# RG-LRU scan and soft mixture of experts: the input gate of the first four token blocks by tanh, their product on VectorE, and a new instruction order

## The chip, the cores and the metric

One core of a Trainium2 chip runs the whole program. The metric is device microseconds from launch to end. Engines are named as the profile names them: PE is TensorE, DVE is VectorE, ACT is ScalarE, POOL is GpSimd, and SP is the queue that issues the DMAs.

## The reference, cut to what matters

```python
# x, r_gate, i_gate: (4, 5056, 256) float32; a_param: (256,)
a_base = 1 / (1 + exp(-a_param))
sig_r, sig_i = sigmoid(r_gate), sigmoid(i_gate)
a_t  = exp(8 * sig_r * log(a_base))
norm = sqrt(maximum(1 - a_t * a_t, 1e-6))
x_gated = norm * sig_i * x
for t in range(S):                      # a linear recurrence along each sequence
    h = a_t[:, t] * h + x_gated[:, t];  y[:, t] = h
# soft mixture of experts over the N = 20224 tokens of y: 8 experts, 4 slots each
logits = y @ phi                        # (N, 32)
slots = softmax_over_tokens(logits).T @ y
slot_out[e] = relu(slots[e] @ w1[e]) @ w2[e]
out = softmax_over_slots(logits) @ slot_out
```

## The kernel before

The 20224 tokens are cut into 40 blocks of 512 (the last has 256). A block lies in memory with tokens on the partitions, and the scan wants channels there, so PE transposes. What is done for block w, with its name in the plan and the line that does it in the profile:

- `Lr`, `Li`, `Lx`: SP loads r, i and x, 512 KB each (L382).
- `rp`, `sr`: PE transposes r, four transposes for each half of the channels (L397); ACT takes the gate from PSUM (L409).
- `si`: ACT takes the input gate in place, untransposed (L420).
- `ex`: ACT makes a = exp(8 sig_r log a_base) (L462, or L460 where the gate was a sigmoid).
- `sq`, `qr`: POOL squares a (L471), 128x1024 in SBUF; ACT takes the root of 1 - a*a (L478).
- `u`: POOL multiplies gate and x (L432), 128x1024, both operands in SBUF.
- `up`, `st`, `sc`: PE transposes that product (L490); DVE multiplies it in PSUM with the root, held at 1e-3 or more (L500), and scans (L513); each for the two halves.
- `yp`, `yc`: PE transposes y back (L533), and DVE or ACT copies it out of PSUM (L288 on DVE, L286 on ACT).

Logits and the running softmax over tokens follow for each four blocks. After the last block come the sum of the slots, the experts (PE, weights loaded during the first part), and for every token the softmax over slots, the product with the slots' outputs (L894), the copies (L288, L286), and the write of 20.7 MB (L912).

ACT works on **units** of one or two blocks: `si`, `ex` and `qr` are each done once for a unit. The functions lie in three tables, sigmoid, exponential and root; tanh is to be had with the sigmoid and with the exponential. The gate of r is written for both: as a sigmoid while the sigmoid's table is in force, else as tanh(r/2) with the half put into `ex`. `TANH_I` lists the units whose input gate is done likewise; it is empty here. The branch for it is in the code (`twice`): the gate is tanh(i/2), which may run in the exponential's phase; the product is (1 + tanh) * x, one DVE instruction that reads two tiles in SBUF; this is twice the product wanted, so the root is taken of 0.25 - 0.25 a*a, and its floor is halved.

Nothing at run time sets the order. `ORDER` is a list of 1243 numbers: the operations in the order in which they are emitted, a `b` choosing the second engine where two are possible. Each engine, and SP, works off its own in that order. The buffers are given out by `Plan.take` along the same list: SBUF has 38 for tiles of 512 KB (a unit of two blocks takes a pair), PSUM has eight banks. An operation that takes a buffer waits until the last operation on its former content is done; on SP, all later loads wait behind it.

Of the kernel before, what the change touches and what calls it, by code (L numbers as in the profile page):

```python
# [26 lines left out]


ORDER = """
# [15 lines left out]
507 431 592 508 529 299b 852 530 531 532 611 613 612 614 472 858 509 510 318 354 376 373 355 377 391 411 432 452  # L45
473 392 493 320 337 359 339 319 321 859 374 361 340 360 362 338 465 487 424 464 627 486 446 648 730 415 378 380
393 412 381 396 860 861 733 653 397 413 398 862 394 416 430 711 587 609 505 527 506 528 451 379b 433 474 470 395
417 414 492 471 713 630 631 654 712 714 511 864 865 437 456 871 872 438 457 439 453 434 632 478 873 458 435 454
436 479 455 866 735 867 875 868 475 595 633 736 513 734 876 863 869 418 399 401 459 461 419b 402b 460b 554 476
480 477 651 420 497 870 400 462 498 421 512 533 516 481 519 483 482 499 494 596 514 534 616 652 874 555 575 515  # L50
597 556 495 484 496 877 878 879 538 880 520 440 441 517 442 535 882 536 518 521 443 539 540 537 881 522 667 500
883 670 502 668 588 610 628 546 689 568 975 672 649 789 811 547 569 552 553 690 629 650 989 749 770 523b 634 671
593 541 574 503 884 501 557 560 816 561 543 562 558 544 886 792 542b 673 674 692 576 693 559 594 885 793 887 598
579 601 635 615 655 752 888 889 890 753 580 602 581 577 603 599 578 775 694 794 620 891 621 600 622 717 776 817
814 795 695 773 774 815 617 563 565 566 676 618 892 619 604 582 893 584 583 894 524 638 636 656 637 718 738 677
697 585 895 606 657 641 605b 525b 607b 564b 719 678 660 754 623 897 625 639 658 642 640 710 709 731 669 732 691
790 812 963 986 965 750 771 969 985 751 772 643 661 659 662 675 715 696 682 679 904 905 626 680 683 906 716 756
898 755 737 757 701 908 698 681 684 699 702 700 703 723 720 899 900 739 901 902 624b 798 685 686b 663 664b 909
704 644 705b 665 687 646 896 645b 666b 688b 647b 758 778 759 721 724 722 725 740 799 819 800 742 743 741 903 910
760 911 706 912 707 744 915 913 763 916 726 745 777 779 782 761 764 762 796 747 917 919 765 780 783 781 784 746b  # L60
727b 748b 766 768 728 1089 767b 920 918 729b 978 977 966 791 971 813 979 962 987 983 968 959 957 797 801 804 921
818 820 922 923 924 823 805 802 907 769b 914 803 806 974 972 961 824 821 825 822 982 981 958 988 960 967 976 973
964 980 984 970 785 1067 926 927 786b 807 928 787 937 938 808b 929 788 930 939 946 931 826 827b 940 947 809 810b
941 932 933 942 948 949 943 934 944 935 1090 950 1068 925 951 945 936 952 1013 1111 1035 953 1177 954 1091 990
1112 1113 1000 1114 991b 1036 1014 1037 1038 1039 995 992 996 1005 1001 997 1002 993 1069 1015 1070 1115 1016
1006 1092 998 1071 1017 994 1003 999 1007 1008 1004 1009 1178 1093 1179 1010 955 1116 1040 1018 1094 1072 1041
956 1011 1073 1042 1074 1180 1012b 1055 1056 1057 1059b 1058b 1043 1049 1044 1047 1050 1053 1046b 1045b 1061
1095 1052b 1065b 1096b 1062b 1063b 1051 1181 1064 1075 1076b 1077b 1079 1078 1082 1199 1019 1083b 1086b 1084b
1085 1200 1020 1201 1182 1104 1155 1105b 1107 1156 1097 1157 1133 1108b 1202 1106b 1098b 1099b 1028 1029b 1032b
1031b 1117 1101 1100 1134 1135 1030 1118b 1021 1022b 1024b 1136 1158 1119 1221 1183 1120b 1184b 1122b 1123b 1025  # L70
1023 1121 1159 1160 1126 1161 1127b 1162b 1129b 1128b 1222 1223 1130 1137 1185 1186 1203 1170 1189b 1187b 1188b
1138 1192 1171 1174b 1173b 1224 1172b 1193 1204 1196 1139 1163 1140b 1194b 1195b 1148 1164 1167 1165 1225 1149
1150 1205 1226 1151b 1152b 1166 1206b 1214 1215 1218 1217 1216b 1060 1048 1054 1066 1227 1228b 1141 1207 1208b
1209b 1210b 1142 1143 1145 1211 1144 1229 1236 1230 1231 1237 1240 1233 1239 1238b 1232b 1080 1081 1087 1088
1110 1103 1109 1033 1102 1034 1026 1124 1027 1125 1131 1132 1175 1191 1190 1176 1153 1197 1168 1220 1219 1147
1213 1198 1242 1234 1235 1146 1154 1212 1169 1241
"""


# [11 lines left out]
class Plan:  # L91
# [84 lines left out]
def kernel(  # L176
# [56 lines left out]
    def Bk(key):  # L233
        return banks[plan.place[key]]
# [4 lines left out]
    def halves(key):  # L239
        return G(key).rearrange("p (h t) -> p h t", h=H)  # L240
# [116 lines left out]
    def window(w):  # L357
# [136 lines left out]
                    )  # L494
            return emit

        def e_st(h):
            def emit(o):
                up = Bk(("up", w, h))[:, :c]
                nc.vector.scalar_tensor_tensor(  # L500
                    up, halves(("N", w))[:, h, :c], 5e-4 if twice else 1e-3, up, op0=ALU.max, op1=ALU.mult
                )
            return emit

        cuts = [0] + [b * S - w * C for b in range(1, B) if w * C < b * S < w * C + c] + [c]

        def e_sc(h):
            def emit(o):
                up = Bk(("up", w, h))
                for s0, s1 in zip(cuts[:-1], cuts[1:]):  # L510
                    init = 0.0 if (w * C + s0) % S == 0 else last_col[h]
                    dst = halves(("A", w))[:, h, s0:s1]
                    nc.vector.tensor_tensor_scan(  # L513
                        dst, dst, up[:, s0:s1], init, op0=ALU.mult, op1=ALU.add
                    )
                    last_col[h] = halves(("A", w))[:, h, s1 - 1 : s1]
            return emit

        for h in range(H):
            op(("up", w, h), "PE", 0.5 * f, e_up(h), deps=[("u", w), ("ident",)],  # L520
               alloc=[("B", ("up", w, h))], uses=[("x", w)])
            op(("st", w, h), "DVE", 0.06 + 0.54 * f, e_st(h), deps=[("up", w, h), ("qr", u0)],
               uses=[("N", w), ("up", w, h)])
            op(("sc", w, h), "DVE", 0.09 * (len(cuts) - 1) + 1.09 * f, e_sc(h),
               deps=[("st", w, h), ("sc", w - 1, h)],
               uses=[("A", w), ("up", w, h)] + ([("A", w - 1)] if w else []))

        def e_yp(i):
            def emit(o):
# [436 lines left out]
```

## Time and profile before

| | |
|---|---|
| median of 3 runs | 301.55 us (301.49 to 302.47) |
| the profiled execution | 301.67 us, span of its instructions 299.8 us |
| busy in the span | PE 234.7, DVE 239.7, ACT 242.2, POOL 181.9 us |
| bytes moved | 100.03 MB, mean 334 GB/s |
| ACT table loads | 24 |

The profile is of one execution. Busy time is a share of the whole span, but the span has three parts: blocks come in and are scanned, up to about 216 us; the experts, to about 245 us; and the output, to the end. Lines that are not quoted in the prediction are left out here.

### The profile page before, as it was taken

The numbers are of one execution on the slowest core, as the hardware profiler recorded it, in microseconds if no ns is written. First come the engines' busy times: TensorE is split into PE (matmuls) and PEld (weight loads), VectorE is DVE, ScalarE is ACT, GpSimd is POOL, SyncE is SP. The second block draws the span as 40 slices with busy tenths as digits, with TensorE's granted clock in tenths as the row PEclk, the third lists the DMA queues.
The fourth block names the chain that finished last, engine by engine and source line by source line (L and its number), as shares of the span: only waits on it lengthen the run. The fifth ranks groups of instructions, "written<-read, shape, count | busy, mean of one in ns | idle before, by whom it ended". The sixth has DMA issues, their size and how long they took to land.

```text
span 299.8 us, 5788 instructions
## 1 busy us (share of the span) xinstructions
PE 234.7 (78%) x2140; PEld 166.0 (55%) x2140; DVE 239.7 (80%) x379; ACT 242.2 (81%) x303; POOL 181.9 (61%) x122
## 2 busy tenths in 40 slices
PE   3605788869896989799958996899999999898200
PEld 3505575666773967457647663557573677665100
DVE  1003999899999999989999999999968779889600
ACT  5899999999999999999999999999323248885100
POOL 4299579988498898899749898798000421121000
PEclk9975999979999899979999999999999999999755
DMA  6999999799895988859998789999991019999997
GB/s 247 416 410 407 410 397 382 306 390 359 327 416 206 416 340 330 302 200 382 331 360 318 273 302 404 385 378 380 339 398 60 3 79 402 404 402 407 404 378 297
DMA packets 28032, 100.03 MB, mean 334 GB/s; under 512 B 3362, under 2 KB 3364, under 8 KB 28004
## 3 DMA queue, kind: packets, MB, share of 16 engines
q1 hardware_dynamic: 28004, 99.66, 86.7%
q8 instruction: 17, 0.28, 0.4%
q14 instruction: 11, 0.09, 0.1%
HBM read 78.94 MB, written 20.71 MB: 332 GB/s over the span
## 4 chain that ended last, share of the span: by engine, by line
ACT 28%; PE 27%; POOL 15%; issue 12%; DVE 7%; DMA 4%; DVEq 0%; POOLq 0%; ACTq 0%
POOL g L471 8%; POOL g L432 5%; ACT g L462 4%; ACT g L420 4%; ACT g L478 4%; PE b L397 4%; ACT y L286 4%; ACT g L409 4%; PE b L894 4%; DMA g<-in_x_dram 4%; PE b L533 3%; PE b L490 3%; DVE g L288 3%; PE b L788 2%; PE b L761 2%
## 5 line engine op out<-in xcount | busy, mean ns | idle before, releaser
L432 POOL TENSOR_TENSOR g<-g 128x1024 f32<-128x1024 f32 (+1 forms) x40 | 92.7, 2344 | 18.9 <-ACT g L420 17.2
L513 DVE TENSOR_TENSOR_SCAN g<-g,b 128x512 f32<-128x512 f32 (+4 forms) x86 | 98.7, 1175 | 0.4
L471 POOL TENSOR_TENSOR g<-g 128x1024 f32<-128x1024 f32 (+1 forms) x40 | 73.8, 1873 | 17.9 <-ACT g L462 13.6
L500 DVE SCALAR_TENSOR_TENSOR b<-g,b 128x512 f32<-128x512 f32 (+1 forms) x80 | 51.8, 675 | 25.1 <-PE b L490 24.1
L490 PE MATMUL b<-ident,g 128*128 128x128 f32 x316 | 48.5, 289 | 22.0 <-POOL g L432 20.2
L490 PEld LDWEIGHTS b<-ident,g 128*128 128x128 f32 x316 | 36.3, 146 | 35.0 <-POOL g L432 23.6
L397 PE MATMUL b<-ident,g 128*128 128x128 f32 x316 | 46.7, 293 | 6.0 <-DMA g<-in_r_gate_dram 3.7
L533 PE MATMUL b<-ident,g 128*128 128x128 f32 x316 | 44.7, 284 | 8.3 <-DVE g L513 6.8
L397 PEld LDWEIGHTS b<-ident,g 128*128 128x128 f32 x316 | 37.9, 151 | 15.7 <-issue 4.2
L533 PEld LDWEIGHTS b<-ident,g 128*128 128x128 f32 x316 | 35.8, 144 | 18.8 <-DVE g L513 11.2
L409 ACT ACTIVATE g<-b 128x512 f32<-128x512 f32 (+1 forms) x80 | 42.4, 604 | 2.9 <-PE b L397 2.9
L861 POOL TENSOR_TENSOR y<-y,rs 128x512 f32<-128x512 f32 x10 | 10.4, 1047 | 53.5 <-DVE g L779 25.2
L462 ACT ACTIVATE g<-g,ca 128x1024 f32<-128x1024 f32 (+2 forms) x30 | 39.1, 1371 | 0.0
L420 ACT ACTIVATE g<-g 128x2048 f32<-128x2048 f32 (+2 forms) x22 | 37.9, 1744 | 0.1
L478 ACT ACTIVATE g<-g 128x2048 f32<-128x2048 f32 (+2 forms) x22 | 36.8, 1732 | 0.1
L288 DVE COPY y<-b 128x512 f32<-128x512 f32 x53 | 34.6, 680 | 2.1 <-PE b L533 1.5
L286 ACT COPY g<-b 128x512 f32<-128x512 f32 (+1 forms) x45 | 22.2, 567 | 8.7 <-PE b L894 8.0
L894 PE MATMUL b<-soR,y 32*128 32x256 f32 x320 | 27.2, 405 | 1.2 <-ACT y L286 0.7
L288 DVE COPY g<-b 128x512 f32<-128x512 f32 (+1 forms) x43 | 24.7, 629 | 2.5 <-ACT y L286 0.8
L286 ACT COPY y<-b 128x512 f32<-128x512 f32 x36 | 20.0, 601 | 5.7 <-PE b L533 4.4
L621 PE MATMUL b<-y,e 128*32 128x257 f32 x316 | 22.9, 388 | 1.2 <-ACT e L612 1.2
L579 PE MATMUL b<-g,phi_sb 128*32 128x512 f32 (+1 forms) x160 | 22.4, 622 | 0.0
(86 smaller groups left out, 220.2 us busy)
## 6 DMA issues: line engine op xcount, KB each, us to landing
g<-in_i_gate_dram SPq DMA_DIRECT2D x39, 512.0 KB, 7.1
g<-in_x_dram SPq DMA_DIRECT2D x39, 512.0 KB, 6.5
out_dram<-g SPq DMA_DIRECT2D x39, 512.0 KB, 6.4
g<-in_r_gate_dram SPq DMA_DIRECT2D x38, 512.0 KB, 6.5
g<-in_moe_w_dram SPq DMA_DIRECT2D x32, 512.0 KB, 6.2
g<-in_r_gate_dram SPq DMA_DIRECT2D x3, 256.0 KB, 5.0
g<-in_i_gate_dram SPq DMA_DIRECT2D x1, 256.0 KB, 4.2
g<-in_x_dram SPq DMA_DIRECT2D x1, 256.0 KB, 7.7
```

Source lines behind the costliest of these rows:

```text
L286: nc.scalar.copy(out=dst, in_=srct)
L288: nc.vector.tensor_copy(out=dst, in_=srct)
L397: nc.tensor.transpose(out=by_tile(rp, n)[:, j, :], in_=rows(("r", w), n)[:, j, h * P : (h + 1) * P], identity=ident,)
L409: nc.scalar.activation(halves(("A", w))[:, h, :c], Bk(("rp", w, h))[:, :c], f, scale=k)
L420: nc.scalar.activation(a, a, AF.Tanh if twice else AF.Sigmoid, scale=0.5 if twice else 1.0)
L432: nc.gpsimd.tensor_tensor(out=rows(("x", w), n), in0=rows(("i", w), n), in1=rows(("x", w), n), op=ALU.mult)
L462: nc.scalar.activation(a, a, AF.Exp, scale=ca[:, h : h + 1], bias=ca[:, h : h + 1])
L471: nc.gpsimd.tensor_tensor(out=halves(("N", w))[:, :, :c], in0=a, in1=a, op=ALU.mult)
L490: nc.tensor.transpose(out=by_tile(up, n)[:, j, :], in_=rows(("x", w), n)[:, j, h * P : (h + 1) * P], identity=ident,)
L500: nc.vector.scalar_tensor_tensor(up, halves(("N", w))[:, h, :c], 5e-4 if twice else 1e-3, up, op0=ALU.max, op1=ALU.mult)
L513: nc.vector.tensor_tensor_scan(dst, dst, up[:, s0:s1], init, op0=ALU.mult, op1=ALU.add)
L533: nc.tensor.transpose(out=yp[:, j, h * P : (h + 1) * P], in_=halves(("A", w))[:, h, (2 * i + j) * P : (2 * i + j + 1) * P], identity=ident,)
```

## The change

The units are now {0}, {1}, {2, 3}, {4, 5} and so on in twos; before they were {0}, {1, 2}, {3, 4}, {5}, {6, 7} and so on. The first three, blocks 0 to 3, have their input gate by tanh: `si` runs in the exponential's phase, `u` is one DVE instruction for each block, and `qr` carries the quarter. A path that would put the floor and the product with the root on POOL (`BY_POOL`) is written in and used for no block. `ORDER` is new throughout. The lines move: L429 is the product on DVE, L433 POOL's, L410 the gate of r, L421 `si`, L463 `ex`, L472 the square, L479 the root, L491 `up`, L504 `st`, L528 `sc`, L289 the copy on DVE.

```diff
-UNITS = [1] + [2] + [2, 1] + [2] * 17
-TANH_I = []
+UNITS = [1, 1] + [2] * 19
+TANH_I = [0, 1, 2]
 EXM = [(12, 14), (18, 20), (30, 34), (36, 38)]
+BY_POOL = []
 ORDER = """
-5 1 33 55 11 115 74 96 116 34 13 56 12 75 97 138 35 137 57 178 200 76 159 98 219 241 160 179 201 117 0 3 6 7 8 9
...
+5 1 0 3 6 7 8 9 10 11 14 16 15 12 18 17 33 36 38 37 39 20 55 58 96 60 99 101 77 82 80 118 121 59 100 102 83 42
...
+        pooled = w in BY_POOL
+        least = 5e-4 if twice else 1e-3
+
         def e_st(h):
...
-                    up, halves(("N", w))[:, h, :c], 5e-4 if twice else 1e-3, up, op0=ALU.max, op1=ALU.mult
+                    up, halves(("N", w))[:, h, :c], least, up, op0=ALU.max, op1=ALU.mult
...
+            if pooled:
+                continue
```

The new order at the places that the prediction speaks of (`g` is a tile in SBUF, `b` a bank of PSUM, `ca` the constants of the channels). ACT from its last `ex` ahead of the first root, before (the r gate's tanh of block 4 is L409 here, `ex` of blocks 3 and 4 the second L462):

```order
L409 ACTIVATE g<-b_73 128x512
L462 ACTIVATE g<-g,ca 128x512 x2
L462 ACTIVATE g<-g,ca 128x2x512 x2
L420 ACT_TABLE_LOAD
L420 ACTIVATE g<-g 128x1024
L420 ACTIVATE g<-g 128x2048
L478 ACT_TABLE_LOAD
L478 ACTIVATE g<-g 128x1024
L478 ACTIVATE g<-g 128x2048
L420 ACT_TABLE_LOAD
```

and the same place now (L463 is `ex`, L421 `si`, L479 `qr`; the first L463 here is blocks 2 and 3, the last blocks 4 and 5):

```order
L410 ACTIVATE g<-b_74 128x512
L463 ACTIVATE g<-g,ca 128x2x512 x2
L421 ACTIVATE g<-g 128x1024
L421 ACTIVATE g<-g 128x2048
L463 ACTIVATE g<-g,ca 128x2x512 x2
L479 ACT_TABLE_LOAD
L479 ACTIVATE g<-g,quarter 128x1024 x2
L479 ACTIVATE g<-g,quarter 128x2048
L479 ACTIVATE g<-g 128x2048
L421 ACT_TABLE_LOAD
```

The load of the sigmoid's table ahead of the first root is gone; the gates of block 1 and of blocks 2 and 3 stand among the exponentials (block 0's is the second ACT instruction after the constants), and the roots of blocks 0 to 5 follow each other as before.

DVE from its first instruction on a block, before (the 128x512 with a bank `b` are `st`, L500, and `sc`, L513, which is listed under the name of its kind):

```order
L334 TENSOR_SCALAR ca<-ca 128x2
L500 SCALAR_TENSOR_TENSOR b_72<-g,b_72 128x512
L500 SCALAR_TENSOR_TENSOR b_73<-g,b_73 128x512
L513 SCALAR_TENSOR_TENSOR g<-g,b_73 128x512
L513 SCALAR_TENSOR_TENSOR g<-g,b_72 128x512
L500 SCALAR_TENSOR_TENSOR b_76<-g,b_76 128x512
```

and now:

```order
L335 TENSOR_SCALAR ca<-ca 128x2
L429 SCALAR_TENSOR_TENSOR g<-g 128x1024 x4
L504 SCALAR_TENSOR_TENSOR b_74<-g,b_74 128x512
L504 SCALAR_TENSOR_TENSOR b_76<-g,b_76 128x512
L528 SCALAR_TENSOR_TENSOR g<-g,b_74 128x512
L504 SCALAR_TENSOR_TENSOR b_73<-g,b_73 128x512
```

The four products, of blocks 0, 2, 3 and 1 in this order, stand ahead of every `st`, so a late product is a late scan.

POOL from its first square, before (L471 the squares of blocks 1, 2, 0, 5 and 3, L432 the products):

```order
L471 TENSOR_TENSOR g<-g 128x1024 x5
L432 TENSOR_TENSOR g<-g 128x1024 x2
L471 TENSOR_TENSOR g<-g 128x1024
L432 TENSOR_TENSOR g<-g 128x1024 x6
L471 TENSOR_TENSOR g<-g 128x1024 x6
```

and now (L472 the squares of blocks 0 to 3, then 4 and 5; six small memsets stand between):

```order
L472 TENSOR_TENSOR g<-g 128x1024 x4
L297 MEMSET y_62 128x4
...
L472 TENSOR_TENSOR g<-g 128x1024 x2
L433 TENSOR_TENSOR g<-g 128x1024 x4
L472 TENSOR_TENSOR g<-g 128x1024 x6
```

POOL has four products fewer, and its last squares of this stretch, blocks 2 to 5, fall into the time of DVE's products.

On SP the loads begin r0, i0, r1, r2, r4, r3, r5, r6, i1, x2, i2, i3, x0, r8, x3, x1, r7, r14, i4 (the number is the block); before they began r1, r2, r0, r5, r3, r4, i5, i1, x0, i2, i0, i3, i4, i6, x1. By the buffers that `Plan.take` gives out, i4 and i5 go to the pair that held i2 and i3, which `u` of blocks 2 and 3 read last; before, none of the first 29 loads waited for a product. In the first part DVE makes 48 of the 79 copies `yc` and ACT 31; before it was 50 and 29. The table loads are 23.

More of the change, by code (lines that the diff above doesn't have):

```diff
@@ L50 @@
[L50 to L64, printed above, removed]
@@ new lines @@
+453 454 458 692 865 875 671 633 693 713 714 513 672 554 673 863 874 876 734 494 475 455 495 476 477 496 533 512
+866 867 868 497 478 479 480 869 399 516 401 418 420 514 534 595 421b 515 555 575 556 596 616 597 498 870 402 440
+442 459 400 419 460 461 499 443 877 878 879 880 462 881 441 519 520 517 518 481 694 483 484 538 882 539 521 883
+535 500 501 502 536 668 547 588 690 610 546 587 628 609 568 649 789 811 629 569 540 537 884 792 749 669 650 770
+552 553 560 557 503b 593 793 695 482b 634 814 541 574 576 579 886 752 542b 674 561 558 559 577 562 578 594 598
@@ new lines @@
+664b 646 647b 626b 685 687 688b 909 907 666b 706 707b 739 742 721 725 686 722 740 743 741 744 758 778 759 799
+819 777 800 796 760 910 763 911 912 913 914 915 916 761 764 762 917 745 726 728 779 747 782 919 765 780 783 781
+784 727b 729b 746b 1089 766 768 920 918 748b 769b 767b 988 989 967 791 979 959 970 977 960 975 962 984 966 981
+813 963 987 797 801 804 818 957 802 805 803 921 922 923 924 820 785 787 806 821 823 824 825 822 926 1067 927 928
+807 937 938 1090 939 946 925 1068 971 976 958 964 968 985 961 974 978 980 965 982 788b 786b 808b 826 930 931 827
@@ new lines @@
+941 947 809 810b 948 932 933 949 934 929 942 935 1091 950 940 951 936 943 944 945 952 1177 1111 1013 953 1035
+1069 1178 954 990 995 991 1179 1036 1112 1014 1015 1180 996 1000 992 997 993 1005 1113 1114 1001b 994 1037 998
+1038 1006 1181 1007 1002 1003 1008 999 1004 1009 1070 1016 1092 1093 1071 1039 1115 1010 955 956 1072 1040 1094
+1041 1011 1012b 1073 1074b 1042 1043 1044b 1047 1045 1046b 1055 1061 1056b 1058b 1059 1057 1063 1065 1049 1053
+1062b 1052b 1064b 1050b 1095 1017 1051 1096b 1075 1076b 1077b 1079 1078 1116 1018 1082 1133 1083b 1086b 1085b
@@ new lines @@
+1084 1134 1199 1135 1200 1104 1105 1107 1019 1117 1136 1137 1106b 1020b 1108b 1118b 1201 1097 1098b 1101b 1221
+1138 1182 1139 1140b 1099 1100 1222 1223 1028 1202 1029b 1031b 1030 1032 1126 1141 1127 1128 1130b 1129b 1203
+1119 1142b 1145b 1224 1143b 1144 1155 1120 1156 1157 1204 1205 1122b 1225 1226 1206b 1121b 1123b 1021 1148 1022b
+1149b 1024 1152b 1227 1183 1228b 1025 1151 1150 1023 1184b 1158 1214 1215 1217 1218b 1216b 1207 1048 1060 1066
+1054 1208 1209 1210b 1211b 1185 1236 1186b 1188 1187 1237 1189b 1240b 1229 1159 1238 1230 1231 1239 1232b 1233b
@@ L77 @@
+1160 1161 1192 1162b 1193b 1195b 1170 1194b 1196 1163 1171b 1173b 1172b 1174 1164 1165b 1166b 1167b 1081 1080
+1087 1088 1110 1109 1103 1102 1034 1132 1131 1033 1147 1124 1146 1125 1154 1026 1219 1212 1220 1190 1153 1235
+1213 1198 1234 1242 1241 1176 1168 1027 1197 1169 1175 1191
 """
@@ L500, in emit, with e_uc, e_nm, e_pb @@
                 nc.vector.scalar_tensor_tensor(
-                    up, halves(("N", w))[:, h, :c], 5e-4 if twice else 1e-3, up, op0=ALU.max, op1=ALU.mult
+                    up, halves(("N", w))[:, h, :c], least, up, op0=ALU.max, op1=ALU.mult
                 )
             return emit
+        def e_uc(h):
+            return lambda o: copy(o, halves(("x", w))[:, h, :c], Bk(("up", w, h))[:, :c])
+        def e_nm(o):
+            nt = halves(("N", w))[:, :, :c]
+            nc.gpsimd.tensor_scalar(nt, nt, least, None, op0=ALU.max)
+        def e_pb(o):
+            b = halves(("x", w))[:, :, :c]
+            nc.gpsimd.tensor_tensor(out=b, in0=halves(("N", w))[:, :, :c], in1=b, op=ALU.mult)
         cuts = [0] + [b * S - w * C for b in range(1, B) if w * C < b * S < w * C + c] + [c]
@@ L526, in window @@
                uses=[("A", w), ("up", w, h)] + ([("A", w - 1)] if w else []))
+        if pooled:
+            op(("nm", w), "POOL", 0.08 + 0.95 * f, e_nm, deps=[("qr", u0)], uses=[("N", w)])
+            for h in range(H):
+                op(("uc", w, h), ("ACT", "DVE"), {"DVE": 0.06 + 0.54 * f, "ACT": 0.055 + 0.43 * f}, e_uc(h),
+                   deps=[("up", w, 0), ("up", w, 1)], uses=[("x", w), ("up", w, h)])
+            op(("pb", w), "POOL", 0.08 + 1.77 * f, e_pb, deps=[("nm", w), ("uc", w, 0), ("uc", w, 1)],
+               uses=[("N", w), ("x", w)])
+            for h in range(H):
+                op(("sc", w, h), "DVE", 0.09 * (len(cuts) - 1) + 1.09 * f, e_sc(h),
+                   deps=[("pb", w), ("sc", w - 1, h)], uses=[("A", w), ("x", w)] + ([("A", w - 1)] if w else []))
         def e_yp(i):
```

29 lines of the change are left out of this document (10 added, 19 removed), and 29 rows, old and new, of the table ORDER.

## The prediction

> **What bounds the kernel now.** I first read the page: span, busy time of each engine, the 40 slices, and the chain that ended last.
>
> ```profile
> span 299.8 us, 5788 instructions
> ...
> DVE  1003999899999999989999999999968779889600
> ACT  5899999999999999999999999999323248885100
> ...
> DMA  6999999799895988859998789999991019999997
> ...
> ACT 28%; PE 27%; POOL 15%; issue 12%; DVE 7%; DMA 4%; DVEq 0%; POOLq 0%; ACTq 0%
> ```
>
> The slices show three stretches, so I cut the span at their borders with the table of windows (columns: window, its length, busy time and instructions of each engine, granted PE clock, DMA share, GB/s).
>
> ```profile
> 0.00:27.50 27.50, 9.62 (x59) 8.91 (x60) 0.98 (x5) 23.21 (x30) 17.42 (x38) 0.83 0.94 367
> 27.50:216.00 188.50, 164.23 (x1406) 118.04 (x1405) 183.50 (x251) 183.01 (x200) 154.08 (x75) 0.97 0.92 347
> 216.00:245.00 29.00, 28.55 (x329) 16.63 (x329) 21.09 (x60) 9.48 (x21) 5.16 (x5) 1.00 0.35 132
> 245.00:299.80 54.80, 32.34 (x352) 22.41 (x350) 34.10 (x66) 26.53 (x54) 5.23 (x5) 0.83 0.97 379
> ```
>
> Once DVE has its first block (27.5 us) it is busy 183.5 of 188.5 us, and ACT 183.0. Neither has more than 5.5 us to give in seven parts of the span out of ten. The last 55 us belong to the DMA (0.97), the 29 before to PE (28.55), and the change touches neither. So the change is worth what it does to two moments: when DVE can begin its steady work, and when ACT begins its own; then whatever either is spared or given until 216 us.
>
> What sets the beginning is told by the chain of work between 12 and 33 us (start, length, what):
>
> ```profile
> 18.47 1.89 POOL g L471
> ...
> 20.73 1.89 POOL g L471
> ...
> 23.10 1.77 POOL g L432
> ...
> 25.41 2.35 POOL g L432
> ...
> 29.57 2.38 POOL g L432
> ```
>
> Squares and products on POOL are the early chain; the change takes four products out of it. On ACT the same stretch reads, in the timeline (start, length, what; in brackets the idle time ahead and who ended it):
>
> ```profile
> 6.83 0.60 ACT L409 ACTIVATE g<-b 128x512 f32<-128x512 f32 x1 [0.26 <-PE b L397]
> 8.37 2.07 ACT L409 ACTIVATE g<-b 128x512 f32<-128x512 f32 x4 [0.94 <-PE b L397]
> 10.29 2.39 ACT L462 ACTIVATE g<-g,ca 128x1024 f32<-128x1024 f32 x2
> ...
> 14.44 2.55 ACT L409 ACTIVATE g<-b 128x512 f32<-128x512 f32 x5
> 16.83 3.82 ACT L462 ACTIVATE g<-g,ca 128x512 f32<-128x512 f32 x4
> 20.67 1.28 ACT L420 ACT_TABLE_LOAD   x1
> 21.96 2.86 ACT L420 ACTIVATE g<-g 128x1024 f32<-128x1024 f32 x2
> 24.84 1.28 ACT L478 ACT_TABLE_LOAD   x1
> 26.13 5.61 ACT L478 ACTIVATE g<-g 128x1024 f32<-128x1024 f32 x4
> 31.75 1.28 ACT L420 ACT_TABLE_LOAD   x1
> 33.05 1.91 ACT L420 ACTIVATE g<-g 128x2048 f32<-128x2048 f32 x1
> ```
>
> ACT works without a gap from 8.4 us on; its roots start at 26.13 and its steady work, the next gates, at 33.05.
>
> **The change part by part: ACT up to the roots.** Ahead of the first root the order now has 13 takings of r's gate instead of 12: one more by (2.55 - 0.60) / 4 = 0.49. It has the input gates of four blocks instead of three, one more by half of 1.91, 0.95. The exponentials are for six blocks as before. One table load goes, -1.28. The waits of 0.26 and 0.94 fall at another place: block 0's input gate, about 1 us of work, now stands in one of them, so I take half of the 1.20 away, -0.60, with 0 and -1.20 as ends. Sum: 26.13 + 0.49 + 0.95 - 1.28 - 0.60 = 25.7 for the first root. Backward from there: the last exponentials end at 24.4, begin 2.3 earlier (22.1, from 2.39 for such a pair), the gates of blocks 2 and 3 begin at 20.2, block 1's at 19.2. So the exponentials of blocks 2 and 3 end at 19.2.
>
> The Trainium skill ("ScalarE: Activation LUTs", section on what ACT_TABLE_LOAD costs) adds a drain of about 1.38 us to the 1.28 of a switch. The trace does not show it: the load of 20.67 ends at 21.95 and the next instruction starts at 21.96. By the page the load that goes would be worth 1.4 us more, and the first root would come at 24.3.
>
> **The loads.** SP's issues of the first loads follow each other as here, and the first transposes start at 4.85:
>
> ```profile
> 13.96 0.33 SPq L382 DMA_DIRECT2D g<-in_r_gate_dram  x1
> 15.23 0.33 SPq L382 DMA_DIRECT2D g<-in_x_dram  x1
> ...
> 4.85 3.37 PE L397 MATMUL b<-ident,g 128*128 128x128 f32 x15 [2.46 <-DMA g<-in_r_gate_dram]
> ```
>
> A load each 1.27 to 1.28 us, so the n-th can be used at 4.85 + 1.28 (n - 1). In the new order x2 is the 10th, x0 the 13th, x3 the 15th, x1 the 16th: 16.4, 20.2, 22.8, 24.05.
>
> **The product on DVE.** No instruction of this form and size is in the trace. The same operation from PSUM, the scan, the copy on DVE, and the two operations of POOL, by the table of groups (busy, mean ns of one):
>
> ```profile
> L500 DVE SCALAR_TENSOR_TENSOR b<-g,b 128x512 f32<-128x512 f32 x78 | 51.1, 682 | 25.1 <-PE b L490 24.1 <-ACT g L478 0.7 <-ACT g L409 0.3
> L500 DVE SCALAR_TENSOR_TENSOR b<-g,b 128x256 f32<-128x256 f32 x2 | 0.7, 414 | 0.0
> L513 DVE TENSOR_TENSOR_SCAN g<-g,b 128x512 f32<-128x512 f32 x72 | 89.9, 1268 | 0.4
> ...
> L432 POOL TENSOR_TENSOR g<-g 128x1024 f32<-128x1024 f32 x39 | 91.5, 2371 | 18.9 <-ACT g L420 17.2 <-ACT g L409 1.4 <-DMA g<-in_x_dram 0.3
> L471 POOL TENSOR_TENSOR g<-g 128x1024 f32<-128x1024 f32 x39 | 72.8, 1894 | 17.9 <-ACT g L462 13.6 <-ACT g L409 1.8 <-DVE b L500 1.7
> ```
>
> From 256 to 512 elements costs 0.268, so 1024 cost 0.682 + 2 x 0.268 = 1.22, the low end; two scans, 2.5, are the high one. I take 1.22, since L500 is the same operation. Four are 4.9 us, against 4 x 2.37 = 9.5 spared on POOL. They lie in a time in which DVE does nothing (0.98 us busy up to 27.5), so by themselves they cost nothing, if they are done when the first `st` can start. In this DVE timeline that was at 27.57:
>
> ```profile
> 27.57 1.29 DVE L500 SCALAR_TENSOR_TENSOR b<-g,b 128x512 f32<-128x512 f32 x2 [23.59 <-PE b L490]
> ...
> 32.33 0.68 DVE L288 COPY y<-b 128x512 f32<-128x512 f32 x1
> 32.93 1.27 DVE L513 TENSOR_TENSOR_SCAN g<-g,b 128x512 f32<-128x512 f32 x1
> ```
>
> **The product against POOL's squares.** The product reads two tiles in SBUF while POOL squares in SBUF. Before has one place where a DVE instruction with two SBUF inputs, L857, falls into POOL's work; its ten by line, and the place in the timeline:
>
> ```profile
> L857 DVE SCALAR_TENSOR_TENSOR rs<-rs x10: 174/175/459, 230.8 to 271.3; 128x16 f32<-128x16 f32 x10
> ...
> 233.79 2.05 POOL L861 TENSOR_TENSOR y<-y,rs 128x512 f32<-128x512 f32 x2 [24.71 <-DVE g L779]
> ...
> 234.41 0.46 DVE L857 SCALAR_TENSOR_TENSOR rs<-rs 128x16 f32<-128x16 f32 x1
> ```
>
> The median is 0.175; this one took 0.459 and ended at 234.87, just behind the end of the first POOL instruction (half of 2.05 after 233.79: 234.8) and 0.98 ahead of the second's end. So DVE stood until POOL's instruction was done, and was served ahead of the next one. Taken over to the products this is a turn about: a square of 1.89, a product of 1.22, a square, and so on. Bounds from both sides: no blocking (that one case being chance), and full turns.
>
> By turns: square 2 from 19.3 to 21.2; product 0 (ready at 20.2) to 22.4; square 3 to 24.3; product 2 to 25.5; square 4 to 27.4; product 3 to 28.6; square 5 to 30.5; product 1 to 31.7. All four products stand ahead of the first `st`, which so starts at 31.8 instead of 27.57: +4.2 on DVE, and PE's transposes and every scan wait with it. DVE makes two copies fewer later, each 32.93 - 32.33 = 0.60: -1.2. DVE's side: +3.0.
>
> ACT's side by turns: roots 0, 1 and 2 with 3 last to 25.7 + 2 x 1.0 + 1.9 = 29.6; root 4 with 5 waits for square 5, 30.6 to 32.5; load to 33.8; gates at 33.8 instead of 33.05, +0.75. Behind that ACT has one taking (0.49) and one block's gate (0.95) less to do, and two copies more, each priced as a taking (0.49): -0.5. But load i4, the 19th, takes the buffers of i2 and i3, and SP holds it, with all loads behind it, until product 3 is done: 28.6 instead of 24.6 if nothing blocks. Loads come 4 us later, the r gates among them, so ACT can lose up to 4.0 - 0.5 = 3.5. Between 3.0 on DVE and 3.5 on ACT I take 3.2, as both engines carry the stretch; nothing covers it, since each has but 5 us idle in 188.
>
> Sum against the profiled execution's own 301.67 us (0.12 above the median): 301.67 + 3.2 = 304.9.
>
> The Trainium skill ("SBUF — State Buffer", section "SBUF: two separate sides") states that a DVE instruction with two SBUF inputs and a GpSimd instruction that reads SBUF share a port pair under an exclusive lock: who starts first holds it for the whole instruction, and the other fully blocks. By that rule a long product also blocks a square, which the 0.175 us instruction is too short to show; it says nothing on who is next when both wait. With the rule the sum is 304.9, without it the 300.3 below.
>
> **The rivals.** *Nothing blocks (faster).* Products 0, 2, 3, 1 end at 21.4, 23.4, 24.6, 25.8; squares 4 and 5 at 26.3 and 28.2. The first `st` waits only for the first root, at 26.8: -0.8, and with the copies -2.0 on DVE. ACT's gates start at 32.9, -0.15 and -0.5 behind it: -0.65. Between them -1.4: 300.3. For it: nine of ten L857 at their length. Against it: none of the nine is known to have met POOL, the tenth did. It decides the sign as long as product 1 ends before 27.57 + 1.2 = 28.8; with one square between any two products it does not.
>
> *DVE keeps its turn.* If back-to-back products are served ahead of a waiting square, products run 21.2 to 26.1 and `st` is in time (-2.0 on DVE); squares 3, 4, 5 end at 28.0, 29.9 and 31.8, root 4 runs 31.9 to 33.8, and the gates start at 35.1: +2.05, less 0.5, +1.5 on ACT. Between -2.0 and +1.5 the later engine counts more, but DVE's lead feeds ACT's idle 5.5; I take +0.8: 302.5. For it: in the L857 case DVE was served ahead of POOL's next. Against it: that was one instruction, not a second in a row.
>
> *The early loss is caught up.* With 5 us idle on DVE after 27.5, a part of +3.2 might be filled by work that now stands ready. If 2 of the 5 are, +1.2: 302.9. Against it: those idle times are spread over 188 us, and order is fixed.
>
> **How the numbers follow.** Chances: turns 0.56, nothing blocks 0.17, DVE keeps its turn 0.20, caught up 0.07. The predicted time is that of turns, 304.9. Its own range is 303.4 (0.6 waits the other way, products on the low side, some idle filled) to 306.8 (products of 1.7 instead of 1.22 us: four times 0.5 more). The range of 8 in 10 takes in the second and fourth case and the edge of the first rival: 300.6 to 306.8. About 0.3% (0.9 us) is what a measurement of this kernel can tell from no change, so faster is below 300.65 and slower above 302.45. Faster: most of the case in which nothing blocks and a little of the third, 0.16. Same: half of DVE's turn, the rest of the first rival, 0.17. Slower: 0.67.
>
> **What the profile would show.** Under turns: L429 with means well over 1.22 (up to 3.1 with the wait, if waiting counts as busy, as it did for L857), ends of product and square that touch, the first L504 near 31.8, and a gap in SP's issues until about 28.6. Without blocking: four L429 at 1.2 each, first L504 at 26.8, squares at 1.89. With DVE's turn: L429 in a row, a square of over 5 us, the L421 of 2048 elements at 35. The first root at 25.7 and 23 loads of 1.28 without a drain check the part on ACT. The forecast is wrong if the squares 3 to 5 come at another time than I put them (exponentials more than 1.5 us earlier would leave fewer turns), if the products are much longer than 1.22, or if the late loads hit another engine harder than ACT.

## The result, and the profile after

The changed kernel takes 311.0 us (median of six runs, 308.86 to 312.26) where the kernel before took 301.59 (301.39 to 302.47) on the same chip: ratio 1.0294, 95% interval 1.0266 to 1.0322. It is 9.4 us slower; 3.2 were forecast. The profiled execution of it took 311.49 us with a span of 309.7, so the differences below are those of the spans, 9.9 us.

Page of the changed kernel, span and slices:

```profile
span 309.7 us, 5799 instructions
...
DVE  1009999989999998989998999999986689999200
ACT  4799949999999999998999899999632437886600
...
DMA  5899789999898978768979579999992009999997
```

I cut both spans at DVE's first work on a block and at the last scan (table of windows, columns as before; the first fence is the kernel before, the second the changed one):

```profile
27.50:215.60 188.10, 163.83 (x1402) 117.64 (x1401) 183.10 (x251) 183.01 (x200) 154.08 (x75) 0.97 0.92 347
215.60:299.80 84.20, 61.29 (x683) 39.44 (x681) 55.59 (x124) 36.00 (x74) 10.39 (x10) 0.89 0.75 293
```

```profile
0.00:33.30 33.30, 15.79 (x81) 13.78 (x81) 10.89 (x9) 26.89 (x33) 17.48 (x37) 0.80 0.83 315
33.30:225.00 191.70, 166.07 (x1381) 118.50 (x1382) 183.93 (x249) 180.97 (x201) 147.60 (x71) 0.95 0.90 339
225.00:309.70 84.70, 60.18 (x679) 40.83 (x678) 53.49 (x119) 37.98 (x78) 10.35 (x10) 0.88 0.74 289
```

The first `st` comes 5.8 us later (33.34 against 27.57). From there to the last scan the changed kernel takes 191.7 instead of 188.1 us, 3.6 more: DVE is busy 0.8 longer, not 1.2 less, and idle 7.8 instead of 5.0. The rest adds 0.5. So nearly four tenths of the loss lie in a stretch to which the forecast had given a gain.

The place that the forecast spoke of most, POOL's squares against DVE's products, one instruction a row (timeline; start, length, idle before):

```profile
21.95 1.89 POOL L472 TENSOR_TENSOR g<-g 128x1024 f32<-128x1024 f32 x1 [2.79 <-ACT g L463]
23.38 1.53 DVE L429 SCALAR_TENSOR_TENSOR g<-g 128x1024 f32<-128x1024 f32 x1 [19.40 <-DMA g<-in_x_dram]
23.80 2.87 POOL L472 TENSOR_TENSOR g<-g 128x1024 f32<-128x1024 f32 x1
24.84 2.91 DVE L429 SCALAR_TENSOR_TENSOR g<-g 128x1024 f32<-128x1024 f32 x1
26.94 2.56 POOL L472 TENSOR_TENSOR g<-g 128x1024 f32<-128x1024 f32 x1
27.67 2.91 DVE L429 SCALAR_TENSOR_TENSOR g<-g 128x1024 f32<-128x1024 f32 x1
29.47 2.87 POOL L472 TENSOR_TENSOR g<-g 128x1024 f32<-128x1024 f32 x1
30.51 2.91 DVE L429 SCALAR_TENSOR_TENSOR g<-g 128x1024 f32<-128x1024 f32 x1
33.34 0.68 DVE L504 SCALAR_TENSOR_TENSOR b<-g,b 128x512 f32<-128x512 f32 x1
```

Read the ends: square to 23.84, product to 24.91, square to 26.67, product to 27.75, square to 29.50, product to 30.58, square to 32.34, product to 33.42. A product ends 1.08 after the square ahead of it, a square 1.75 to 1.76 after the product ahead of it. The lengths of 2.9 hold the wait for the other engine, which the profile counts as busy.

ACT at the start of the changed kernel:

```profile
8.44 1.06 ACT L421 ACTIVATE g<-g 128x1024 f32<-128x1024 f32 x1 [2.51 <-DMA g<-in_i_gate_dram]
...
11.35 1.09 ACT L410 ACTIVATE g<-b 128x512 f32<-128x512 f32 x2 [1.37 <-PE b L398]
...
26.88 1.28 ACT L479 ACT_TABLE_LOAD   x1
28.18 4.08 ACT L479 ACTIVATE g<-g,quarter 128x1024 f32<-128x1024 f32 x3
...
35.59 1.91 ACT L421 ACTIVATE g<-g 128x2048 f32<-128x2048 f32 x1
...
41.74 0.60 ACT L410 ACTIVATE g<-b 128x512 f32<-128x512 f32 x1 [2.29 <-PE b L398]
44.24 1.09 ACT L410 ACTIVATE g<-b 128x512 f32<-128x512 f32 x2 [1.90 <-PE b L398]
```

i0, the second load, came at 8.4, not at 6.1, and the first root at 28.2, not at 25.7. SP's issues (start, length, count) show two holds: nothing is issued between 6.74 and i1 at 14.34, nor between 20.27 and i4 at 27.78, and what follows i4 comes only as products end:

```profile
2.98 3.76 SPq L383 DMA_DIRECT2D g<-in_r_gate_dram  x5
14.34 0.33 SPq L383 DMA_DIRECT2D g<-in_i_gate_dram  x1
...
19.35 0.92 SPq L383 DMA_DIRECT2D g<-in_r_gate_dram  x2
27.78 3.16 SPq L383 DMA_DIRECT2D g<-in_i_gate_dram  x2
33.44 0.33 SPq L383 DMA_DIRECT2D g<-in_x_dram  x1
```

### The profile page after: what moved, and what is told of

Same layout as the page of the kernel before. It is cut to its first block, busy times and chain, and to the rows that moved or that the text cites. A ratio compares the mean times of both kernels' runs of the same rounds, so it can differ in the third digit from the quotient of the medians.

```text
span 309.7 us, 5799 instructions
## 1 busy us (share of the span) xinstructions
PE 242.0 (78%) x2140; PEld 173.1 (56%) x2140; DVE 248.3 (80%) x376; ACT 245.8 (79%) x311; POOL 175.4 (57%) x118
## 4 chain that ended last, share of the span: by engine, by line
PE 29%; ACT 28%; DVE 16%; DMA 10%; issue 7%; SPq 2%; POOL 1%; POOLq 0%; ACTq 0%; DVEq 0%
DMA g<-in_r_gate_dram 8%; ACT g L410 6%; ACT g L463 5%; ACT g L421 4%; PE b L491 4%; PE b L560 4%; PE b L921 4%; DVE g L528 4%; PE b L648 3%; DVE b L504 3%; PE b L398 3%; PE b L606 3%; PE b L788 2%; DMA g<-in_i_gate_dram 2%; ACT g L479 2%
## 5 line engine op out<-in xcount | busy, mean ns | idle before, releaser
L433 POOL TENSOR_TENSOR g<-g 128x1024 f32<-128x1024 f32 (+1 forms) x36 | 83.6, 2341 | 34.4 <-DMA g<-in_x_dram 15.4
L528 DVE TENSOR_TENSOR_SCAN g<-g,b 128x512 f32<-128x512 f32 (+4 forms) x86 | 99.1, 1178 | 0.9
L472 POOL TENSOR_TENSOR g<-g 128x1024 f32<-128x1024 f32 (+1 forms) x40 | 76.4, 1938 | 21.3 <-issue 9.9
L491 PE MATMUL b<-ident,g 128*128 128x128 f32 x316 | 52.9, 303 | 23.1 <-DVE g L429 9.8
L398 PE MATMUL b<-ident,g 128*128 128x128 f32 x316 | 51.5, 308 | 12.6 <-DMA g<-in_r_gate_dram 7.2
L491 PEld LDWEIGHTS b<-ident,g 128*128 128x128 f32 x316 | 38.6, 154 | 37.8 <-POOL g L433 9.4
L504 DVE SCALAR_TENSOR_TENSOR b<-g,b 128x512 f32<-128x512 f32 (+1 forms) x80 | 52.0, 678 | 4.3 <-PE b L491 2.9
L398 PEld LDWEIGHTS b<-ident,g 128*128 128x128 f32 x316 | 40.8, 159 | 22.7 <-DVE g L528 7.9
L410 ACT ACTIVATE g<-b 128x512 f32<-128x512 f32 (+1 forms) x80 | 42.1, 596 | 8.2 <-PE b L398 7.3
L560 PE MATMUL b<-ident,g 128*128 128x128 f32 x316 | 45.2, 281 | 3.3 <-ACT y L287 1.4
L560 PEld LDWEIGHTS b<-ident,g 128*128 128x128 f32 x316 | 34.9, 142 | 15.7 <-ACT y L287 3.0
L421 ACT ACTIVATE g<-g 128x2048 f32<-128x2048 f32 (+2 forms) x22 | 38.0, 1750 | 2.6 <-DMA g<-in_i_gate_dram 2.5
L463 ACT ACTIVATE g<-g,ca 128x1024 f32<-128x1024 f32 (+2 forms) x32 | 39.7, 1305 | 0.0
L479 ACT ACTIVATE g<-g 128x2048 f32<-128x2048 f32 (+2 forms) x19 | 33.2, 1799 | 0.2
L289 DVE COPY y<-b 128x512 f32<-128x512 f32 x49 | 32.0, 680 | 0.8 <-PE b L560 0.6
L287 ACT COPY y<-b 128x512 f32<-128x512 f32 x40 | 21.7, 595 | 9.3 <-PE b L560 5.3
L921 PE MATMUL b<-soR,y 32*128 32x256 f32 x320 | 26.4, 423 | 0.7 <-ACT g L287 0.4
L289 DVE COPY g<-b 128x512 f32<-128x512 f32 (+1 forms) x40 | 23.0, 626 | 4.7 <-PE b L921 3.8
L287 ACT COPY g<-b 128x512 f32<-128x512 f32 (+1 forms) x48 | 23.6, 563 | 3.4 <-PE b L921 3.2
L429 DVE SCALAR_TENSOR_TENSOR g<-g 128x1024 f32<-128x1024 f32 x4 | 10.0, 2564 | 19.4 <-DMA g<-in_x_dram 19.4
```

The source lines that it names most:

```text
L287: nc.scalar.copy(out=dst, in_=srct)
L289: nc.vector.tensor_copy(out=dst, in_=srct)
L398: nc.tensor.transpose(out=by_tile(rp, n)[:, j, :], in_=rows(("r", w), n)[:, j, h * P : (h + 1) * P], identity=ident,)
L410: nc.scalar.activation(halves(("A", w))[:, h, :c], Bk(("rp", w, h))[:, :c], f, scale=k)
L421: nc.scalar.activation(a, a, AF.Tanh if twice else AF.Sigmoid, scale=0.5 if twice else 1.0)
L433: nc.gpsimd.tensor_tensor(out=rows(("x", w), n), in0=rows(("i", w), n), in1=rows(("x", w), n), op=ALU.mult)
```

## Experiments

Each kernel was compared with the kernel before on the chip on which it ran (302.0 to 302.3 us there). The changed kernel's 311.0 was taken beside 301.59, so a difference to it is good to about 0.7 us.

### Squares that read nothing

```diff
         def e_sq(o):
             a = halves(("A", w))[:, :, :c]
+            if 2 <= w <= 5:
+                for _ in range(2):
+                    nc.gpsimd.memset(halves(("N", w))[:, :, :c], 0.5)
+                return
```

> The changed kernel, in which POOL does not square blocks 2 to 5: it fills their tile with a constant, twice, so that it is busy about as long (2 x 0.9 us) but reads nothing from SBUF (the roots of these blocks are left out in this sense). Theory A (a product with two SBUF inputs and a POOL instruction that reads SBUF take turns): L429 falls from 2.9 to 1.1 to 1.2 us each, the last ends near 28, the first L504 waits for the first root alone and moves from 33.3 to about 29.3, i4 is issued near 25 instead of 27.8; time about 306 (305 to 307.5). Rival B (any POOL instruction blocks it, written tiles too): L429 stays near 2.9 or 2.0, the time within 1 us of 311. Rival C (the product itself takes 2.9 us): L429 2.9, 311.

306.0 us (305.0 to 307.2), ratio 1.0142 (1.0103 to 1.0182): 5.0 us less than the changed kernel. The product by line, and POOL's fills:

```profile
L429 DVE SCALAR_TENSOR_TENSOR g<-g x4: 1217/1224/1226, 24.0 to 27.8; 128x1024 f32<-128x1024 f32 x4
...
L474 POOL MEMSET g<- 128x1024 f32 x8 | 7.5, 952 | 0.2
```

All four products take 1.22 us although three of them lie over fills (0.952 each, as many and as long as alone). So the product itself costs 1.22, a fill, which only writes, does not stop it, and a square, which also reads, does. That is theory A. The first `st` came at 29.7. ACT's two waits of 2.29 and 1.90 shrank to one of 0.96: they were the late scans, not loads, as the next run shows. The Trainium skill ("SBUF — State Buffer", section "SBUF: two separate sides") limits the lock for a DVE instruction with two SBUF inputs to a GpSimd instruction that reads SBUF; these rows agree.

### Loads that nothing holds

```diff
+OWN = {('i', 1): 36, ('x', 0): 37, ('i', 4): 34, ('x', 4): 32, ('r', 8): 30, ('r', 10): 28, ('i', 6): 24, ('i', 8): 26}
...
         _, i, f = fit
+        if a[1] in OWN:
+            i = OWN[a[1]]
...
```

> The changed kernel with other buffers for the first loads: i1, x0, r8, r10, i4 with i5, x4, i6 and i8 get buffers that nothing held before, so that none of the first loads waits for a transpose of r or a product (in the changed kernel i1 was held 7.6 us by the transposes of r4, and i4, i5, x4 by the products until 33.4). Theory A (the loss is in two parts, products that take turns with squares, and loads held by buffers): x0 lands 0.9 us earlier, but the products still take turns with the squares, so the first L504 stays within 1 us of 33.3; the two waits of ACT for the r gates at 41 and 44 us (2.3 and 1.9) go, and so do most of the 3.4 us that DVE is idle more; time 306.5 to 308.5. Rival B (the held loads cost nothing of their own): 310.5 to 311.5. Rival C (the held loads are all): below 303.

310.2 us (309.0 to 311.0), ratio 1.0265 (1.0227 to 1.0303): 0.8 less than the changed kernel, within the spread of both. Of theory A the start holds: x0 is there 0.6 us earlier, and the first `st` (L510 here) stands where it stood.

```profile
22.75 10.84 DVE L435 SCALAR_TENSOR_TENSOR g<-g 128x1024 f32<-128x1024 f32 x4 [18.85 <-DMA g<-in_x_dram]
33.51 1.28 DVE L510 SCALAR_TENSOR_TENSOR b<-g,b 128x512 f32<-128x512 f32 x2
```

So x0, which came late in the changed kernel, is not what set the first `st`: the squares did, and they begin when ACT's exponentials are done (the square of block 2 at 21.95 in the changed kernel, 22.11 here). The rest of theory A fails. The loads ran without a hold, and the waits stayed. ACT, then PE in the same stretch:

```profile
41.96 0.60 ACT L416 ACTIVATE g<-b 128x512 f32<-128x512 f32 x1 [2.35 <-PE b L404]
44.08 1.09 ACT L416 ACTIVATE g<-b 128x512 f32<-128x512 f32 x2 [1.52 <-PE b L404]
```

```profile
35.97 0.66 PE L404 MATMUL b<-ident,g 128*128 128x128 f32 x4 [1.67 <-DVE g L534]
37.68 1.11 PE L497 MATMUL b<-ident,g 128*128 128x128 f32 x4 [1.05 <-DVE g L534]
```

ACT waits for PE, and PE waits for scans (L534 here) before its next transposes. A transpose of r (L404) reads nothing that a scan writes, so what it waits for must be its bank of PSUM, which the scan frees. DVE's late start goes round to ACT by PSUM, with all loads in time.

### r0 in one load

```diff
-                cuts = [0, n // 2, n] if (nm, w) == ("r", 0) else [0, n]
+                cuts = [0, n]
```

> The changed kernel with r0 loaded in one piece of 512 KB instead of two of 256 KB. In the changed kernel i0, the second load, landed at 8.4 us, 2.3 later than a load each 1.28 us would give, and DMA moved about 200 GB/s from 4 to 6.5 us. Theory A (the two small loads at the head starve the DMA): i0 lands at 6.1 to 6.6, everything up to the first root is about 2 us earlier (28.2 to 26.2), time about 309. Rival B (the first touch of another tensor, or chance, slows it): i0 still at about 8, the time 310 to 312.

309.1 us (307.8 to 311.6), ratio 1.0252 (1.0195 to 1.0310). ACT's gate of block 0, the first root, and the first `st`:

```profile
6.51 1.05 ACT L421 ACTIVATE g<-g 128x1024 f32<-128x1024 f32 x1
...
25.79 4.08 ACT L479 ACTIVATE g<-g,quarter 128x1024 f32<-128x1024 f32 x3
...
30.95 0.68 DVE L504 SCALAR_TENSOR_TENSOR b<-g,b 128x512 f32<-128x512 f32 x1
```

Two loads of 256 KB at the head of the queue are what delayed i0: ACT takes it at 8.4 to 8.6 us in the three traces with r0 in halves, at 6.4 to 6.6 and without a wait in the three with r0 whole. Why, no run here shows. In one piece, the first root stands at 25.8 (forecast 25.7) and everything to the first `st` comes 2.4 us earlier. The median falls by 1.9 us; with ranges of 3 to 4 us the size of that is rough.

### Both at once

The two edits together:

```diff
+            if 2 <= w <= 5:
+                for _ in range(2):
+                    nc.gpsimd.memset(halves(("N", w))[:, :, :c], 0.5)
+                return
...
+                cuts = [0, n]
```

> The changed kernel with both edits: the squares of blocks 2 to 5 left out (their tile filled with a constant, twice) and r0 loaded in one piece. Theory A (the start and the steady stretch are two losses: from the first L504 to the last scan the changed kernel took 190 to 191.6 us in every variant so far, before 188.0): the first L504 comes at 27.0 to 27.6, as in the kernel before, yet the time is 303 to 304.5, since the new order's steady stretch keeps its 2 us. Rival B (turns and the slow first loads are all of the loss): 300.3 to 302.

306.2 us (305.1 to 306.9), ratio 1.0132 (1.0108 to 1.0156).

```profile
26.89 1.29 DVE L508 SCALAR_TENSOR_TENSOR b<-g,b 128x512 f32<-128x512 f32 x2 [1.22 <-ACT g L483]
```

```profile
26.90:218.60 191.70, 165.22 (x1387) 118.63 (x1387) 183.26 (x248) 184.65 (x203) 147.55 (x71) 0.95 0.90 341
```

The first `st` waits only for the first root now and comes 0.7 us ahead of the kernel before. Yet the last scan ends 3.0 us behind it (218.6 against 215.6), since the stretch between is 191.7 us again. The time is above the ranges of both theories: no gain over the run with the fills alone. The start explains only what the steady stretch lets through.

### The rest of the order, one head on the other's tail

The first 230 operations (the head) in one kernel's order, the others (the tail) in the other's. The diffs are shorthand here; the kernels hold the lists. Tail of before on the changed head, with both edits above:

```diff
-ORDER = changed[:230] + changed[230:]
+ORDER = changed[:230] + [o for o in before if o not in changed[:230]]
```

> The first 230 operations in the changed kernel's order, all others in the order of the kernel before; with the two edits that took the start's loss away (r0 in one piece; the squares of blocks 2 to 5 left out, their tile filled with a constant). With the changed kernel's whole order these two edits gave 306.2 us, though the first L504 came 0.7 us earlier than in the kernel before. Theory A (from the first L504 on it is the new order of the rest that costs, 191.7 instead of 188.0 us to the last scan): with the rest in before's order it is 188 to 189.5 us, the time 301 to 303. Rival B (the squares left out, or the state in which the head leaves buffers and loads, cost it): 305 to 307.

303.7 us (302.7 to 306.8), ratio 1.0077 (1.0048 to 1.0106): 2.5 less than with the changed tail, and between the ranges of the two theories. From the first `st` to the last scan:

```profile
27.10:217.20 190.10, 163.14 (x1392) 117.14 (x1391) 183.46 (x251) 183.84 (x199) 147.23 (x71) 0.97 0.91 345
```

With the changed tail the stretch is 191.7, in the kernel before 188.1. So behind this head the tail accounts for 1.6 of the 3.6 us; the other 2.0 stay with what the head leaves behind, or with the squares left out. No run tells these two apart.

Head of before, tail of the changed kernel, no tanh:

```diff
-ORDER = before[:230] + before[230:]
+ORDER = before[:230] + [o for o in changed if o not in before[:230]]
```

> The reverse: the first 230 operations as in the kernel before, all others in the order of the changed kernel, nothing left out, no tanh. Theory A (the new order of the rest costs 2 to 4 us by itself): first L500 at 27.5 as in the kernel before, time 303.5 to 306. Rival B (the head alone makes the loss): 301 to 302.5.

306.7 us (305.7 to 306.95), ratio 1.0150 (1.0124 to 1.0176).

```profile
27.64 0.70 DVE L500 SCALAR_TENSOR_TENSOR b<-g,b 128x512 f32<-128x512 f32 x1 [23.74 <-PE b L490]
```

```profile
27.60:220.10 192.50, 166.26 (x1405) 117.23 (x1404) 184.47 (x248) 186.23 (x204) 154.25 (x75) 0.97 0.90 341
```

No tanh, no product on DVE, no saved load, the first `st` at its old time, and still 4.4 us more in that stretch (192.5 against 188.1): theory A, with a time 0.7 above its range. The granted PE clock is 0.97 there as in the kernel before, so the lower one of the changed kernel (0.95) is not needed for the loss. Two more runs asked where. Before's order up to block 17:

```diff
-ORDER = before[:230] + [o for o in changed if o not in before[:230]]
+ORDER = before[:480] + [o for o in changed if o not in before[:480]]
```

> The order of the kernel before for the first 480 operations (to the scans of block 17, about 118 us), the changed kernel's order for the others. With 230 operations as before it was 306.7 us, and its scans were 1.3 us late at block 19 (129 us), 3.8 at block 24, 5.3 at block 29. Theory A (the loss of the new order lies in the rows behind 118 us): 305 to 306.5. Rival B (it is in the rows of 60 to 118 us, which come back later as waits): 301.5 to 303.5.

307.8 us (307.4 to 308.0), ratio 1.0185 (1.0132 to 1.0238): the loss stands behind 118 us. It is even 1.0 more, and 1.3 above theory A's range; part of that may be the seam, the place where one order is joined to the other, where DVE is idle 1.5 us at 117. The changed kernel shows the same place without a seam. Its 44th scan of 86 ends at 134.2 us, that of the kernel before at 128.2; from there to the last scan (the kernel before, then the changed one):

```profile
128.20:215.60 87.40, 77.55 (x698) 51.80 (x697) 85.32 (x119) 83.18 (x95) 70.84 (x35) 0.98 0.91 339
134.20:225.00 90.80, 80.41 (x693) 54.49 (x694) 86.96 (x117) 84.99 (x96) 71.76 (x35) 0.94 0.87 332
```

Here lie 3.4 of the 3.6 us: DVE is busy 1.6 longer and idle 1.8 longer. And the copies given back to the engines that made them before, nothing else moved:

```diff
 # the order of the run with 230; engine of each copy of y, a "b" or none
-yc: as in the changed kernel (DVE 48, ACT 31)
+yc: as in the kernel before (DVE 50, ACT 29)
```

> The kernel whose first 230 operations stand as before and the others in the changed kernel's order (306.7 us), in which each copy of y back from PSUM is made by the engine that made it in the kernel before (50 on DVE, 29 on ACT, instead of 48 and 31). From 60 us to the last scan that kernel's ACT had 3 copies and 1 table load more than before (+3.2 us busy), and both its DVE and ACT stood idle more. Theory A (the copies moved to ACT make the new order of the rest longer, ACT being without slack): 304.5 to 305.7. Rival B (what stands in which row of the engines' orders matters, not who copies): 306 to 307.5.

321.7 us (321.5 to 322.0), ratio 1.0651 (1.0605 to 1.0697). Neither theory. 22 copies changed engine in rows that were written for the other engine, which cost 15 us; so this run says nothing of who should copy, only how little such an order bears an edit. It also warns of the seams of the runs above. The stretch of 191.7 us in the changed kernel and in the run with both edits has no seam.

### The idea in the order of the kernel before

```diff
-TANH_I = []
+TANH_I = [0, 1]
```

> The kernel before, in its own order of instructions and loads, with the input gates of blocks 0, 1 and 2 by tanh: their products go to DVE, the table load ahead of the first root goes, POOL has three products fewer. Theory A (turns with squares and the order of loads make the loss, not the idea): no load is held; square 4 and products 0 and 1 take turns (product 0 to 23.7, square 4 to 25.6, product 1 to 26.7), the first L500 at about 26.8 instead of 27.6, ACT's next gates at about 31.8 instead of 33.05, one product of 1.15 us stands in DVE's steady work; time 300 to 301.5. Rival B (a product on DVE costs more than it spares wherever it stands): 303 or more.

301.4 us (300.6 to 303.8), ratio 0.9983 (0.9958 to 1.0009): in theory A's range, but the interval takes in no change.

```profile
20.58 2.90 ACT L420 ACTIVATE g<-g 128x1024 f32<-128x1024 f32 x2
23.49 1.28 ACT L478 ACT_TABLE_LOAD   x1
24.79 3.04 ACT L478 ACTIVATE g<-g,quarter 128x1024 f32<-128x1024 f32 x2
```

```profile
21.71 4.91 DVE L428 SCALAR_TENSOR_TENSOR g<-g 128x1024 f32<-128x1024 f32 x2 [17.57 <-ACT g L420]
26.54 1.28 DVE L500 SCALAR_TENSOR_TENSOR b<-g,b 128x512 f32<-128x512 f32 x2
...
30.11 1.20 DVE L428 SCALAR_TENSOR_TENSOR g<-g 128x1024 f32<-128x1024 f32 x1
```

The saved load brings the first root from 26.13 to 24.79 and the first `st` from 27.57 to 26.54, though two products still take turns with squares (4.91 for both; the third, alone, 1.20). In the profiled execution the gain was gone later, at a load of r:

```profile
77.21 0.70 PE L397 MATMUL b<-ident,g 128*128 128x128 f32 x4 [2.84 <-DMA g<-in_r_gate_dram]
```

I took other buffers for the reason and forced those of the kernel before (`PLACE` lists them):

```diff
-TANH_I = []
+TANH_I = [0, 1]
...
-        _, i, f = fit
+        i = PLACE[a[1]]
...
```

> The kernel before in its own order with the gates of blocks 0 to 2 by tanh and their products on DVE, and with every buffer of SBUF and PSUM as the kernel before has it (the run of that edit with newly given buffers had one gap of 3.1 us on DVE at 77 us, behind a load of r issued at 68.6). Theory A (the gap is from the buffers that the loads were given): the gap is gone, the first L500 stays at 26.5, from there to the last scan 188 to 189 us; time 298.8 to 300.3 where before is 302.0. Rival B (the gap is from products that stand on DVE and POOL's other order): gap as it was, 301 to 302.

301.2 us (300.6 to 304.0), ratio 0.9971 (0.9946 to 0.9995), in the range of rival B, and with the gap at 77 us as it was in the profile; rival B's reason was not tested. PE goes on behind r27 at 76.4 in the kernel before, at 77.2 and 77.8 in these two. From 28 to 90 us the DMA of the kernel before is at 0.97 of its time, so PE, coming earlier, may only wait longer. But both profiles are of long executions (303.8 and 303.35 us, 2.4 and 2.2 above the medians of their kernels), with spans 2.2 and 1.8 us longer than before's, while the medians are shorter than before's. So the usual execution can hardly have a wait of this size, and whether it has a part of it is not shown. To test the place, r27's load was moved ahead of three others:

```diff
 # SP's loads (numbers are blocks)
-r26, x12, x13, r22, r27
+r26, r27, x12, x13, r22
```

> The kernel before with the gates of blocks 0 to 2 by tanh (products on DVE), and the load of r27 moved ahead of those of x12, x13 and r22, right behind r26. In the run without the move the gain of 1 us at the first scan was gone at 77 us, where PE waited 2.8 us for r27 (landed 77.7, in the kernel before 76.4 with a wait of 0.7). Theory A (the first 90 us are bound by the loads, and the order of the loads decides there): r27 lands near 71 to 73, the wait goes, the gain stays; time 299.5 to 300.7. Rival B (the next load takes its place as the wait, as DMA is at 0.97 of its time there): 301 to 302.

300.9 us (300.5 to 302.55), ratio 0.9967 (0.9949 to 0.9986), between the two ranges. It is 1.3 us of medians below the kernel before, the most of all versions here; the run with placed buffers (0.9946 to 0.9995) is the other one whose interval lies below 1. PE's wait for r27 is gone in its profile, which is of an execution at the median. That the move adds to the run without it is not shown, the intervals overlap. The same move in the kernel before, without tanh:

> The kernel before with only that load moved. Theory A: PE's wait of 0.67 at 76.4 goes; 301.0 to 301.8, at most 0.6 us less than before. Rival B: no change or up to 1 us more, since x12, x13 and r22 land 1.3 later each.

302.3 us (301.2 to 302.6), ratio 1.0006 (0.9993 to 1.0018): rival B, it is worth nothing there.

## Why the prediction was wrong, point by point

- **Product, 1.22 us:** right, 1.217 to 1.226 where it met nothing that reads.
- **Turns with the squares:** right in mechanism and sequence. From the first product's start to the last one's end, 10.0 us were measured, where the forecast had 11.5 from 20.2 to 31.7. The first product began later into its square and waited 0.7 less for it, and each of the three turns behind it took 2.84 instead of 1.89 + 1.22 = 3.11.
- **The loads, 4.85 + 1.28 (n - 1):** the first step that failed. The rule came from a queue that begins with whole loads. With r0's halves at the head i0 came 2.3 us late, and ACT's chain with it: the first root at 28.2 instead of 25.7, the square of block 2 at 21.95 instead of 19.3. So the first `st` was at 33.3 instead of 31.8: +5.8 in place of +4.2. I had looked for loads that wait for products only: i1, in r4's buffer, waited for that block's transposes until 14.34, and x0 was there at 23.4 instead of 20.2. That hold did not set the first `st`, as the run without holds shows (33.51).
- **"DVE makes two copies fewer later: -1.2":** the step that made the forecast miss. It priced the whole new order behind the first `st` at its two copies. The two did go (47 copies on DVE up to the last scan, 49 before), but measured was +3.6 there. In the other runs with the changed tail it was +1.9 to +2.8 where one edit was made at the start, +3.6 with turns and r0's halves both away, +4.4 behind the head of the kernel before. With -1.2 to +3.6, and +4.2 to +5.8, the +3.0 on DVE becomes +9.4.
- **Held loads, up to 3.5 us on ACT:** wrong mechanism. i4 was issued at 27.8 (forecast 28.6), but without any hold the time fell by 0.8 only. ACT's loss is DVE's lateness, handed on through PSUM banks and PE.
- **The saved table load, 1.28:** right in size: 1.34 at the first root in the order of before, and no drain (load 23.49 to 24.77, next instruction 24.79), so the trace does not bear out the 2.66 that the Trainium skill gives ("ScalarE: Activation LUTs", section on what ACT_TABLE_LOAD costs).
- **The rival in which nothing blocks, 300.3:** it would have missed too. With nothing blocked and r0 in one load the changed order took 306.2.

Open is what in the rows behind 118 us costs the time, and why the parts do not add up: the changed tail costs 4.4 us behind the head of the kernel before, but 1.6 behind the changed one. Waits of DVE there are short and many, none over 1.1 us in the changed kernel, and no run took one of them apart.

## What to carry to other kernels

A new static order has to be priced over its whole length: where two engines have 5 us idle in 188, any row can cost, and a term of "two copies fewer" is no estimate of a thousand moved instructions. Where an instruction with two SBUF operands goes to VectorE, look what GpSimd reads at that time, and set its time by turns. An earlier start is not an earlier end: with both edits the first `st` came 0.7 us ahead of the kernel before, and the last scan 3.0 us behind it. And before a wait in a profile is called the cause, set the time of the profiled execution beside the median: the waits at 77 us stood in executions 2.2 to 2.4 us above theirs.

## What of the hardware was not expected

- POOL's fills (writes only) and a DVE product with two SBUF inputs run side by side at full speed, 0.952 and 1.22 us; POOL's square, which reads, and the product alternate strictly when both wait, neither engine being served twice in a row.
- Two loads of 256 KB at the head of the DMA queue made the load behind them come about 2 us later than one of 512 KB did (8.4 against 6.5 us at ACT).
